# GpSimd's multiplies and scalings wait, by a semaphore, for VectorE's last one ahead of them

## The chip, the cores and the metric

The kernel runs on one core of a Trainium2 chip. The metric is the device time of one execution in microseconds (us). The core's engines are TensorE (PE in the profile, its weight loads PEld), VectorE (DVE), ScalarE (ACT), GpSimd (POOL) and SyncE (SP), which issues the DMAs. Each engine takes its instructions strictly in the order in which they stand, and halts at one whose semaphores have not reached the counts that it waits for.

## What is computed

One transformer block with modulation, for 2048 tokens of width 512, in bfloat16. The reference, cut to what matters:

```python
mod = (silu(c) @ w_mod).reshape(1, 6, 1, 512)            # sa, ca, ga, sb, cb, gb
h = layernorm(x) * (1 + ca) + sa
q, k, v = split(h @ wqkv)                                # 32 heads of 16
pq, pk = q @ w_phi, k @ w_phi                            # per head, 16 x 16
phi_q = concat([softmax(pq), softmax(-pq)])              # over the 16 features
phi_k = concat([softmax(pk), softmax(-pk)])
kv = einsum('sf,sd->fd', phi_k, v);  z = phi_k.sum(0)    # per head, over all tokens
o = (phi_q @ kv) / (phi_q @ z + 1e-6)
x = x + ga * (o @ wo)
h = layernorm(x) * (1 + cb) + sb
x = x + gb * ((sigmoid(h @ w_gate) * (h @ w_up)) @ w_down)   # 512 -> 1376 -> 512
```

## The kernel before

The 2048 tokens are 16 tiles of 128. For each tile t the first half of the program normalises the tokens (`st1`, `rs1`, `nmr1`, `xn1`), transposes them and applies the modulation (`hm1_gj`: unit g of one or two tiles, quarter j of the width), giving `h1T`. TensorE then makes `K`t and `V`t, and `Q`t, 4 matmuls each, into PSUM banks. The feature map of a K tile is: `e`t, two exponentials on ScalarE (for pk and -pk) from the bank into a buffer; `n`t, the sums on VectorE; `r`t, the reciprocals, on VectorE or ScalarE; `phi`t, the product of the two, on VectorE or GpSimd; then `kv`t on TensorE adds phi times V into two accumulating banks. `va`t copies V out of its bank. Of a Q tile it is `qe`t, `qn`t, two products `qphi`t.0 and `qphi`t.1, and `pT`t, a DMA of SP that transposes the result. The names may have a suffix for a part of a tile.

When all of kv is there, `kvz` and `kvn` on VectorE bring it into SBUF, and each tile goes through `num` (TensorE), `rd` and `u` (VectorE), `oT`, `out` (TensorE), `x1` and the second layer norm, `mod` (the second modulation), and then the gated network in six chunks: `g` and `u` on TensorE, `tg` on ScalarE, `hm` on VectorE, `y` on TensorE, `fin`. `wo`j and `wd`j multiply the weights of the two projections by ga and gb beforehand, with both inputs in SBUF.

Every such step is a task of a graph. The order of all tasks is written out by hand as a text, ORDER, one word for each, with @A, @D or @P where the engine is not the first of its alternatives. `emit` goes through it and records each task on its engine; so the text fixes the order on every engine. The framework adds a semaphore wait wherever data, or the reuse of a buffer, needs one. Buffers are slots by class, handed out in the order of the text: all of `e`, `qe`, `phi` and `qphi` share the class r2k, which has 7 slots. A task that takes over a slot waits for its last reader. PSUM has 8 banks, two of them held by kv until its end.

A task has a `port`: the engines on which it counts as an instruction with two inputs in SBUF, or as a scaling of SBUF data. For `phi`, `qphi`, `wo`, `wd`, `xn1`, `xn2`, `mod` and `hm1` these are VectorE and GpSimd (`hm1` and `mod` only where a DMA did the transposing), for all others GpSimd alone. For instance:

```python
G.add(f"phi{t}.{a}", {"POOL": 0.08 + 1.77 * w, "DVE": 0.16 + 0.54 * w}, f_p, r=[("kr", t, a)], w=[("phi", t, a)], bufs=[ee, kr, ph], port=("POOL", "DVE"))
```

The stretch of ORDER around the first place that the prediction speaks of (`phi4.0` on VectorE stands ahead of `qphi1.1` on GpSimd):

```
K7b qe4.0 n4.0 V6 va6 r4.0@A n5.0 V5 va5 tph81 V4 qn4.0 phi4.0@D qphi1.1@P pT2 r5.0@A va4 qphi1.0@P
```

Of the kernel before, what the change touches and what calls it, by code (L numbers as in the profile page):

```python
# [160 lines left out]
def kernel(  # L161
# [4 lines left out]
    nc = tc.nc  # L166
# [91 lines left out]
    def get(b):  # L258
        if b.tile is None:
            pl = psp if b.cls == "bank" else cst  # L260
            b.tile = pl.tile(b.shape, b.dtype, name=b.name, tag=f"{b.cls}{b.slot}", bufs=1)
        return b.tile
# [5 lines left out]
        return Buf(name if name in CAPS else "ks", shape, FP32, name)  # L268

    def emit(order):  # L270
        for t in order:
            for b in t.bufs:
                if b.cls not in ("h2", "hm", "vaug"):
                    get(b)
            t.fn(t.eng)


    def kv_tasks(G, acc, t, ph, va, parts):
# [598 lines left out]
    bound_tasks(G)  # L877
    downstream(G)
    emit(G.arrange(ORDER))

    def gen_tile(tag, shape, dtype, name):
# [177 lines left out]
```

## Time and profile before

| | us |
|---|---|
| median of 3 runs | 203.47 |
| lowest, highest | 203.35, 204.83 |
| profiled execution, first to last instruction (its span) | 202.2 |
| PE busy, of the span | 194.4 (96%) |
| DVE busy | 160.6 (79%) |
| ACT busy | 105.3 (52%) |
| POOL busy | 104.2 (52%) |

The profile is of one execution. For it the span is what is recorded; the timed runs have their whole time, whose median is 1.27 us above the span. The busy shares are means over the whole span, in which the engines have very different parts: the keys' and queries' features come first, the gated network last. The timeline of an engine gives, for groups of like instructions that follow each other, the start, the time from the first one's start to the last one's end, and in brackets the idle time ahead and what ended it. "L784" is line 784 of the kernel before.

### The profile page before, as it was taken

How to read it: one execution, taken by the hardware profiler on the slowest of the kernel's cores; microseconds unless marked ns; L12 is line 12 of the kernel's file. 1: busy time of each engine (PE TensorE's matmuls, PEld its weight loads, DVE VectorE, ACT ScalarE, POOL GpSimd, SP SyncE). 2: the span in 40 equal slices, each digit the busy share in tenths (PEclk: the TensorE clock that was granted, in tenths of full speed). 3: DMA queues.
4: the chain of work that ended last, by engine and by line, in shares of the span. 5: the costliest groups of instructions: out<-in, count | busy, mean ns of one | idle time of the engine just before them, and what ended most of it. 6: DMA issues, size and time to landing. Idle time of an engine off the chain costs nothing.

```text
span 202.2 us, 4128 instructions
## 1 busy us (share of the span) xinstructions
PE 194.4 (96%) x1447; PEld 106.2 (53%) x1471; DVE 160.6 (79%) x376; ACT 105.3 (52%) x250; POOL 104.2 (52%) x146
## 2 busy tenths in 40 slices
PE   7989999999989999999999999999999999999993
PEld 2545656455464787668844444444444444444442
DVE  3999999999999999998897796885969753326622
ACT  2899999999978975576531215212113420334100
POOL 3889978799699998867570066130030431000000
PEclk9999999999999999999999999999999999999999
DMA  5999965669963992418664243542113031000011
GB/s 169 329 262 239 289 232 111 114 71 261 396 254 77 133 109 51 82 39 108 117 79 80 53 79 85 100 104 52 26 26 81 2 78 54 28 5 26 28 54 57
DMA packets 49452, 22.92 MB, mean 113 GB/s; under 512 B 38065, under 2 KB 47634, under 8 KB 49426
## 3 DMA queue, kind: packets, MB, share of 16 engines
q1 hardware_dynamic: 48896, 22.59, 50.1%
q8 instruction: 12, 0.20, 0.4%
q14 instruction: 14, 0.11, 0.2%
q10 hardware_dynamic: 530, 0.02, 0.2%
HBM read 11.58 MB, written 2.10 MB: 68 GB/s over the span
## 4 chain that ended last, share of the span: by engine, by line
PE 70%; ACT 15%; DVE 8%; issue 2%; POOL 2%; DMA 1%; POOLq 0%; DVEq 0%
PE y_ps L485 19%; PE u_ps L447 18%; PE g_ps L447 18%; PE a_ps L356 5%; ACT h1T L751 3%; ACT e L776 3%; ACT qe L776 2%; PE num L326 2%; PE k_ps L817 2%; DVE qks L780 2%; ACT wqk_f L685 2%; PE v_ps L821 2%; DVE ks L780 1%; DMA x_sb<-in_A_x_dram 1%; DVE phi L787 1%
## 5 line engine op out<-in xcount | busy, mean ns | idle before, releaser
L457 ACT ACTIVATE tg<-g_ps 128x512 bf16<-128x512 f32 (+5 forms) x66 | 28.7, 455 | 66.8 <-PE g_ps L447 39.9
L468 DVE SCALAR_TENSOR_TENSOR wmod_sb<-tg,u_ps 128x512 bf16<-128x512 bf16 (+4 forms) x63 | 30.2, 491 | 18.0 <-ACT tg L457 11.5
L485 PE MATMUL y_ps<-wd_sb,wmod_sb 128*128 128x512 bf16 (+4 forms) x180 | 44.2, 366 | 0.2
L447 PEld LDWEIGHTS <-wg_sb 128*128 128x128 bf16 (+1 forms) x252 | 21.9, 99 | 16.1 <-issue 0.2
L447 PEld LDWEIGHTS <-wu_sb 128*128 128x128 bf16 (+1 forms) x252 | 21.7, 99 | 15.9 <-issue 0.3
L784 POOL TENSOR_TENSOR qphi<-qe,qks 128x512 bf16<-128x512 bf16 x24 | 25.1, 1064 | 4.1 <-DMA pT<-qphi 1.4
L485 PEld LDWEIGHTS <-wmod_sb 128*128 128x128 bf16 (+1 forms) x187 | 17.1, 98 | 16.0 <-issue 0.6
L447 PE MATMUL u_ps<-wT_sb,wu_sb 128*128 128x512 bf16 (+2 forms) x124 | 23.8, 322 | 0.1
L447 PE MATMUL g_ps<-wT_sb,wg_sb 128*128 128x512 bf16 (+2 forms) x122 | 23.0, 321 | 0.2
L447 PE MATMUL g_ps<-wqk_sb,wg_sb 128*128 128x128 bf16 (+4 forms) x127 | 19.9, 287 | 0.1
L447 PE MATMUL u_ps<-wqk_sb,wu_sb 128*128 128x128 bf16 (+4 forms) x127 | 19.8, 286 | 0.2
L780 DVE TENSOR_REDUCE ks<-e 128x64 f32<-128x1024 bf16 (+2 forms) x22 | 19.3, 904 | 0.2
L492 DVE TENSOR_TENSOR ot<-y_ps,x 128x512 bf16<-128x512 f32 (+2 forms) x17 | 11.1, 654 | 10.1 <-PE y_ps L485 10.1
L780 DVE TENSOR_REDUCE qks<-qe 128x64 bf16<-128x1024 bf16 x16 | 19.1, 1204 | 0.0
L376 POOL TENSOR_SCALAR ve<-mv 128x2 f32<-128x2 f32 (+1 forms) x8 | 1.8, 226 | 33.4 <-DVE mv L366 33.3
L776 ACT ACTIVATE e<-k_ps 128x512 bf16<-128x512 f32 (+2 forms) x44 | 18.3, 536 | 0.0
L776 ACT ACTIVATE qe<-q_ps 128x512 bf16<-128x512 f32 x32 | 17.1, 612 | 0.8 <-POOL phi L787 0.6
L787 POOL TENSOR_TENSOR phi<-e,kr 128x1024 bf16<-128x1024 bf16 (+2 forms) x10 | 14.9, 1501 | 2.5 <-DVE phi L787 1.2
L817 PE MATMUL k_ps<-wqk_f,h1T 128*128 128x512 bf16 x61 | 16.1, 379 | 0.1
L356 PE MATMUL a_ps<-wo_sb,oT 128*128 128x512 bf16 x60 | 15.9, 379 | 0.2
L871 PE MATMUL q_ps<-wqk_f,h1T 128*128 128x512 bf16 x61 | 15.7, 379 | 0.2
L821 PE MATMUL v_ps<-wv_sb,h1T 128*128 128x512 bf16 x61 | 15.3, 379 | 0.1
(132 smaller groups left out, 307.7 us busy)
## 6 DMA issues: line engine op xcount, KB each, us to landing
out_dram<-ot SPq DMA_DIRECT2D x15, 128.0 KB, 1.8
x_sb<-in_A_x_dram SPq DMA_DIRECT2D x6, 256.0 KB, 5.1
wmod_sb<-in_w_mod_dram SPq DMA_DIRECT2D x1, 1536.0 KB, 7.0
wu_sb<-in_B_w_up_dram SPq DMA_DIRECT2D x1, 1376.0 KB, 10.9
wg_sb<-in_B_w_gate_dram SPq DMA_DIRECT2D x1, 1376.0 KB, 10.3
wd_sb<-in_B_w_down_dram SPq DMA_DIRECT2D x1, 1280.0 KB, 7.9
wmod_sb<-in_w_mod_dram SPq DMA_DIRECT2D x4, 256.0 KB, 6.2
wqk_sb<-in_A_wqkv_dram SPq DMA_DIRECT2D x2, 256.0 KB, 4.8
```

What stands on the lines that cost most here:

```text
L356: pe.matmul(ap_[:], lhsT=oT[:, j, :], rhs=wo_sb[:, j, :], start=(j == 0), stop=(j == KT - 1))
L447: pe.matmul(ps[:fsz, 0:n], lhsT=w[:, j, ft * P:ft * P + fsz], rhs=h[:, j, 0:n], start=(j == 0), stop=(j == KT - 1))
L457: G.add(f"tg{k}.{ft}", {"ACT": 0.13 + n * 0.00083}, lambda e, tg=tg, g_ps=g_ps, fsz=fsz, n=n: act.activation(tg[:fsz, 0:n], g_ps[:fsz, 0:n ...
L468: dve.scalar_tensor_tensor(hm_all[:fsz, hm[k].slot, ft, 0:n], tg[:fsz, 0:n], 1.0, u_ps[:fsz, 0:n], op0=ALU.add, op1=ALU.mult)
L485: mm = pe.matmul(y[:, 0:c1 - c0], lhsT=hm_all[:fsz, hm[k].slot, ft, tl * P:(tl + 1) * P], rhs=wd_sb[:fsz, ft, c0:c1], start=(ft == 0), sto ...
L776: act.activation(ee[:, a:b, s].rearrange("p g f h -> p g (f h)"), kp[:, a * 64:b * 64].rearrange("p (g n) -> p g n", n=64), ACT.Exp, scale ...
L780: dve.tensor_reduce(ks[:, a:b].rearrange("p g s h -> p (g s) h"), ee[:, a:b].rearrange("p g s f h -> p (g s) h f"), axis=AX.X, op=ALU.add)
L784: engine(e).tensor_tensor(ph[:].rearrange("p (g s f h) -> p g s f h", s=2, f=DH, h=4)[:, :, s], ee[:, :, s], ks[:, :, 1 - s].unsqueeze(2). ...
L787: engine(e).tensor_tensor(ph[:, a * P:b * P].rearrange("p (g f h) -> p g f h", f=DH, h=4), ee[:, a:b].rearrange("p g s f h -> p (g s) f h" ...
L817: pe.matmul(kp[:], lhsT=h1T[:, j, t * P:(t + 1) * P], rhs=wqk_f[:, j, D:2 * D], start=(j == 0), stop=(j == KT - 1))
L821: pe.matmul(vp[:], lhsT=h1T[:, j, t * P:(t + 1) * P], rhs=wv_sb[:, j, :], start=(j == 0), stop=(j == KT - 1))
L871: pe.matmul(qp[:], lhsT=h1T[:, j, t * P:(t + 1) * P], rhs=wqk_f[:, j, 0:D], start=(j == 0), stop=(j == KT - 1))
```

## The change

`emit` remembers the last instruction of the last task that went to VectorE with VectorE in its `port`. Ahead of each task of GpSimd with GpSimd in its `port` (but for the small `rs` tasks), it adds a dependency of that task's first instruction on the remembered one. No instruction is added, removed or moved on any engine.

```diff
     def emit(order):
+        last = None
         for t in order:
             for b in t.bufs:
                 if b.cls not in ("h2", "hm", "vaug"):
                     get(b)
+            body = nc.cur_bb.bb.instructions
+            n0 = len(body)
             t.fn(t.eng)
+            if t.eng in t.port and not t.name.startswith("rs"):
+                if t.eng == "DVE":
+                    last = body[-1].name
+                elif last:
+                    tc.add_manual_dep(body[n0], last, mybir.DependencyInfo(mybir.DependencyClass.Sync, mybir.DependencyReason.DATA), reason="port order")
```

VectorE raises its semaphore as it goes on, and GpSimd's tasks wait for a count of it. Where an earlier wait of GpSimd already covers the new dependency, nothing is added. In the built program nine instructions are left whose count is new or higher:

| GpSimd's instruction | its start in the profile before | now waits for VectorE's | which ran |
|---|---|---|---|
| qphi1.1 | 33.43 | phi4 | 36.78 to 37.46 |
| hm1_73 | 43.35 | phi7 | 43.89 to 44.57 |
| wo1 | 49.02 | phi10 | last of three, to 51.34 |
| wo0 | 56.56 | phi12 | to 55.70 |
| mod21 | 87.36 | qphi10.0 | 86.24 to 86.65 |
| xn2_6 | 91.57 | xn2_7 | 91.25 to 91.80 |
| qphi8.1 (second of the pair) | 101.7 | qphi13.0 | 102.53 to 103.05 |
| mod51 | 132.01 | mod50 | 132.97 to 133.32 |
| mod80 (last of four) | 167.2 | mod71 | 166.70 to 167.34 |

GpSimd's row at the first place, before. qphi_800 is the product of tile 1's query, qphi_821 that of tile 4, h1T the modulated input of tiles 10 to 13, phi_833 the feature map of tile 5:

```order
L784 TENSOR_TENSOR qphi_800<-qe_700,qks_755 128x8x64 [waits DVE_49,Activation_49]
L784 TENSOR_TENSOR qphi_800<-qe_700,qks_755 128x8x64
L753 TENSOR_SCALAR h1T_73<-h1T_73,modc_78 128x256 [waits DMAHW2_49,DMAHW1_49]
L753 TENSOR_SCALAR h1T_73<-h1T_73,modc_78 128x256
L784 TENSOR_TENSOR qphi_821<-qe_766,qks_796 128x8x64 [waits DVE_49,PE_49,Activation_49]
L787 TENSOR_TENSOR phi_833<-e_708,kr_804 128x1024 [waits DMAHW4_49,PE_49,Activation_49]
```

And after the change:

```order
L792 TENSOR_TENSOR qphi_800<-qe_700,qks_755 128x8x64 [waits DVE_49,Activation_49]
L792 TENSOR_TENSOR qphi_800<-qe_700,qks_755 128x8x64
L761 TENSOR_SCALAR h1T_73<-h1T_73,modc_78 128x256 [waits DMAHW2_49,DMAHW1_49]
L761 TENSOR_SCALAR h1T_73<-h1T_73,modc_78 128x256
L792 TENSOR_TENSOR qphi_821<-qe_766,qks_796 128x8x64 [waits PE_49,Activation_49]
L795 TENSOR_TENSOR phi_833<-e_708,kr_804 128x1024 [waits DMAHW4_49,PE_49,Activation_49]
```

The wait on VectorE's semaphore at the first row had the count 76 and has the count 80 now, that of phi4; qphi_821, which waited for 80 by itself, is covered by it. Nothing else differs in these rows.

ScalarE's row of e6, the exponentials of tile 6, the same before and after: it takes over the slot of qe_700, and its wait on GpSimd's semaphore (Pool) is for the second qphi_800. ScalarE's e7 takes over the slot of qphi_800 itself, and so waits for the DMA pT1 that reads it. The bank that e6 reads, k_ps_739, is taken over by V9.

```order
L776 ACTIVATE e_837<-k_ps_739 128x8x64 [waits Pool_49]
L776 ACTIVATE e_837<-k_ps_739 128x8x64
```

GpSimd's rows at the second and third place, before. The first h1T here is hm1_73, wo_sb is wo1, and phi_1094 belongs to tile 14:

```order
L753 TENSOR_SCALAR h1T_73<-h1T_73,modc_78 128x256
L787 TENSOR_TENSOR phi_959<-e_857,kr_880 128x1024 [waits PE_49,Activation_49,Pool_49]
L787 TENSOR_TENSOR phi_986<-e_872,kr_936 128x1024 [waits DMAHW3_49,DVE_49,Pool_49]
L787 TENSOR_TENSOR phi_1015<-e_875,kr_938 128x256 [waits DVE_49,Pool_49]
L851 TENSOR_TENSOR wo_sb_68<-wo_sb_68,ga_sb_102 128x512 [waits DMAHW1_49,DMAHW0_49]
L787 TENSOR_TENSOR phi_1094<-e_912,kr_994 128x512 [waits DMAHW5_49,DVE_49]
```

And after the change:

```order
L761 TENSOR_SCALAR h1T_73<-h1T_73,modc_78 128x256 [waits DVE_49]
L795 TENSOR_TENSOR phi_959<-e_857,kr_880 128x1024 [waits PE_49,Activation_49,Pool_49]
L795 TENSOR_TENSOR phi_986<-e_872,kr_936 128x1024 [waits DMAHW3_49,DVE_49,Pool_49]
L795 TENSOR_TENSOR phi_1015<-e_875,kr_938 128x256 [waits DVE_49,Pool_49]
L859 TENSOR_TENSOR wo_sb_68<-wo_sb_68,ga_sb_102 128x512 [waits DMAHW1_49,DMAHW0_49,DVE_49]
L795 TENSOR_TENSOR phi_1094<-e_912,kr_994 128x512 [waits DMAHW5_49,Activation_49]
```

The wait for phi10 has moved from phi_1094 to wo1, which stands one ahead of it, and hm1_73 has a wait where it had none.

## Prediction

> **What bounds the kernel now.** I read the page first, then the busy times by stretch, then the timelines of each engine between 30 and 58 us, where the change has its first effect. The engines' busy times, and two stretches (length, then PE, PEld, DVE, ACT and POOL busy, clock, DMA share, GB/s):
>
> ```profile
> PE 194.4 (96%) x1447; PEld 106.2 (53%) x1471; DVE 160.6 (79%) x376; ACT 105.3 (52%) x250; POOL 104.2 (52%) x146
> ```
>
> ```profile
> 38.00:43.00 5.00, 4.94 (x38) 2.42 (x38) 4.93 (x7) 4.97 (x13) 4.80 (x4) 1.00 0.60 78
> 58.00:200.00 142.00, 139.68 (x942) 75.94 (x955) 106.93 (x253) 52.98 (x114) 56.29 (x73) 1.00 0.35 66
> ```
>
> TensorE is the bound from end to end: from 58 to 200 us it is idle for 2.32 of 142 us, so what is lost ahead of 58 us can't be made up behind it. In the stretch from 38 to 43 us there is no spare engine at all: PE, DVE and ACT are each busy for over 4.9 of 5 us, POOL for 4.8. An engine that halts here passes its halt to the others. That GpSimd is only 52% busy over the span says nothing about this stretch.
>
> **Which added waits hold anything.** Nine instructions of GpSimd get a condition that no earlier wait of theirs covers. GpSimd's timeline (start, time, line, instruction, count, idle time ahead) at the first three:
>
> ```profile
> 33.43 2.08 POOL L784 TENSOR_TENSOR qphi<-qe,qks 128x512 bf16<-128x512 bf16 x2 [0.84 <-DVE qphi L784]
> 35.49 1.10 POOL L753 TENSOR_SCALAR h1T<-h1T,modc 128x256 bf16<-128x256 bf16 x2
> 37.64 1.20 POOL L784 TENSOR_TENSOR qphi<-qe,qks 128x512 bf16<-128x512 bf16 x1 [1.05 <-DVE phi L787]
> 38.80 1.91 POOL L787 TENSOR_TENSOR phi<-e,kr 128x1024 bf16<-128x1024 bf16 x1
> ...
> 43.35 0.56 POOL L753 TENSOR_SCALAR h1T<-h1T,modc 128x256 bf16<-128x256 bf16 x1
> 44.22 4.84 POOL L787 TENSOR_TENSOR phi<-e,kr 128x1024 bf16<-128x1024 bf16 x3 [0.30 <-PE kvacc L282]
> 49.02 1.22 POOL L851 TENSOR_TENSOR wo_sb<-wo_sb,ga_sb 128x512 bf16<-128x512 bf16 x1
> 51.42 3.06 POOL L787 TENSOR_TENSOR phi<-e,kr 128x512 bf16<-128x512 bf16 x3 [1.18 <-DVE phi L787]
> ```
>
> The first row, the fifth and the seventh are the ones that wait (the pair of qphi1, hm1_73, wo1). Of VectorE they now wait for the phi at 36.78, the one at 43.89 and the last of the three from 50.26; with those, the instructions that the working needs:
>
> ```profile
> 36.78 0.68 DVE L787 TENSOR_TENSOR phi<-e,kr 128x1024 bf16<-128x1024 bf16 x1
> ...
> 38.48 2.34 DVE L780 TENSOR_REDUCE ks<-e 128x64 f32<-128x1024 bf16 x2
> ...
> 43.89 0.68 DVE L787 TENSOR_TENSOR phi<-e,kr 128x1024 bf16<-128x1024 bf16 x1
> ...
> 48.87 0.33 DVE L787 TENSOR_TENSOR phi<-e,kr 128x256 bf16<-128x256 bf16 x1
> ...
> 50.26 1.08 DVE L787 TENSOR_TENSOR phi<-e,kr 128x256 bf16<-128x256 bf16 x3
> ...
> 54.05 0.33 DVE L798 RECIPROCAL kr<-ks 128x32 bf16<-128x32 f32 x1
> ```
>
> **First wait: qphi1 on GpSimd waits for phi4 on VectorE.** The pair at 33.43 must now wait until the phi that starts at 36.78 is done. That phi doesn't depend on the pair, so its time stays. It already released a GpSimd instruction, the one at 37.64; the pair will start there instead: 37.64 - 33.43 = 4.21 us later. GpSimd's idle 1.05 us ahead of 37.64 is used up by this, but its 2.08 and 1.10 us of work now come behind the phi. The first qphi at 37.64 lasted 1.20 beside VectorE's qphi instead of its usual half of 2.08, so the pair ends at 37.64 + 1.16 (to the next start, 38.80) + 1.04 = 39.84, where it ended at 35.51.
>
> Who waits for the pair: ScalarE's exponentials e6, which write the buffer that the pair read (its slot is shown with the change, above), and all that stands behind them. ScalarE's and TensorE's timelines:
>
> ```profile
> 36.90 1.09 ACT L776 ACTIVATE e<-k_ps 128x512 bf16<-128x512 f32 x2
> ...
> 39.81 1.12 ACT L776 ACTIVATE e<-k_ps 128x512 bf16<-128x512 f32 x2
> ```
>
> ```profile
> 37.92 0.42 PE L282 MATMUL kvacc<-vaug,phi 128*128 128x68 bf16 x8
> 38.17 1.89 PE L821 MATMUL v_ps<-wv_sb,h1T 128*128 128x512 bf16 x8
> ...
> 43.88 1.02 PE L817 MATMUL k_ps<-wqk_f,h1T 128*128 128x512 bf16 x4
> ...
> 57.38 0.80 PE L326 MATMUL num<-kvb,pT 128*128 128x68 bf16 x20 [0.43 <-DVE kvb L294]
> ```
>
> e6 started at 36.90; it will start at 39.84 and a handover (0.08 from 51.34 to 51.42, the ends of two rows above), so 3.0 us later, and end at 41.0 instead of 37.99. V9, at 38.17, writes the bank that e6 reads out: TensorE, which takes its instructions in order, halts there for 41.05 - 38.17 = 2.9 us. VectorE's sum of e6 started at 38.48, 0.49 after e6 was done; it loses 3.0 - 0.49 = 2.5 us at once, and the rest with the following sums, since ScalarE has no gap in which to catch up. The halt is thus 3.0 us on all three, 2.5 if VectorE alone counted.
>
> The queue of SP is also behind the pair: the transposing DMA of qphi1, and all that SP issues after it.
>
> ```profile
> 35.53 1.23 SPq L874 DMA_TRANSPOSE pT<-qphi  x1
> ```
>
> ```profile
> DMA to landing us min/median/max: 3.2/3.3/3.9
> ```
>
> It goes out at 39.88 instead of 35.53 and lands 3.2 later, at 43.1. The exponentials e7 reuse its source buffer: they start at 39.81, with the shift 42.81, so they wait 0.3 more. **3.3 us** by now.
>
> **Second wait: hm1_73 waits for phi7 on VectorE.** GpSimd went from its phi straight to hm1_73 at 43.35; the phi of VectorE ends at 44.57. GpSimd is then 3.0 behind, VectorE 3.3, so hm1_73 starts at 44.57 + 3.3 + 0.15 (a handover like that to 37.64) = 48.0 and not at 46.4. Of the 1.6 us, the idle 0.30 ahead of 44.22 takes some, and GpSimd is about 4.4 behind. TensorE's K at 43.88 reads hm1_73 with its last quarter (at 44.53): ready at 48.6, so TensorE stands 4.1 back there, which it partly makes up later, as it isn't what the num at 57.38 waits for. VectorE's phi at 48.87 waits for the second of GpSimd's three phis from 44.22, which by its share of the elements (4.84 x 2 / 2.25 = 4.3) ends at 48.5: slack 0.4. It is thus pushed by 4.4 - 0.4 = 4.0, against 3.3: 0.7 more, of which I take 0.2 off, since the first of the three overlaps VectorE's phi from 43.89 now and won't then: **0.5 us**.
>
> **Third wait: wo1 waits for phi10 on VectorE.** wo1 filled GpSimd's idle time ahead of 51.42, where the next phi was released by the very phi that wo1 now waits for (50.26 + 1.08 = 51.34). Now wo1's 1.2 us come between. Two of GpSimd's three phis from 51.42 are done after 3.06 x 2/3 = 2.04, at 53.46; VectorE's reciprocal at 54.05 waits for them with a slack of 0.59: 1.2 - 0.6 = **0.6 us** more. From there VectorE sets the num at 57.38 (the wait named in its row), and PE halts until it comes.
>
> **The later waits.** At 56.56 the wo0 is ready late anyway, and the mod at 87.36 finds its VectorE instruction done. The others hold GpSimd for 0.1 to 1.4 us:
>
> ```profile
> 100.69 2.08 POOL L784 TENSOR_TENSOR qphi<-qe,qks 128x512 bf16<-128x512 bf16 x2 [0.58 <-POOL wT_sb L424]
> ...
> 132.01 1.73 POOL L424 TENSOR_SCALAR wqk_sb<-wqk_sb,modc 128x256 bf16<-128x256 bf16 x3 [1.42 <-issue]
> ```
>
> ```profile
> 102.53 0.52 DVE L784 TENSOR_TENSOR qphi<-qe,qks 128x512 bf16<-128x512 bf16 x1
> ```
>
> ```profile
> 132.97 0.35 DVE L422 TENSOR_SCALAR wqk_sb<-wqk_sb,modc 128x256 bf16<-128x256 bf16 x1
> ```
>
> ```profile
> 109.49 0.44 PE L326 MATMUL num<-kvb,pT 128*128 128x68 bf16 x8
> 135.50 1.03 PE L447 MATMUL g_ps<-wqk_sb,wg_sb 128*128 128x512 bf16 x4
> ```
>
> The second qphi8 at 101.7 waits until 103.05: 1.4 later, out at 104.2, landed by 108.1 at the slowest, and its reader comes at 109.49. The three mods from 132.01 wait until 133.32: done at 135.1, their reader comes at 135.50. I take both at nothing; if the covers were gone they would cost 0.3 each.
>
> **What the waits save.** VectorE sometimes finds GpSimd on the port. Its qphi and its mod, over the whole program (min/median/max ns):
>
> ```profile
> L784 DVE TENSOR_TENSOR qphi<-qe,qks x8: 415/416/518, 32.5 to 114.0; 128x512 bf16<-128x512 bf16 x8
> ```
>
> ```profile
> L422 DVE TENSOR_SCALAR wqk_sb<-wqk_sb,modc x1: 347/347/347, 133.0 to 133.0; 128x256 bf16<-128x256 bf16 x1
> L422 DVE TENSOR_SCALAR wT_sb<-wT_sb,modc x1: 637/637/637, 166.7 to 166.7; 128x256 bf16<-128x256 bf16 x1
> ```
>
> One qphi in eight is longer, by 0.10 us; one mod by 0.29. With as much for the forms not shown, 0.5 us at most, nearly all behind 58 us where PE is full without it: I take 0. The Trainium skill's page "SBUF — State Buffer", section "Who interferes with whom", states that a VectorE instruction with two SBUF inputs or in a 2-port mode and a reading GpSimd instruction exclude each other for the whole instruction, whoever starts first. The rows agree in kind, and by the rule alone this change should win; by these rows the sum would be 4.4 - 0.5 = 3.9.
>
> **Sum.** 3.0 + 0.3 + 0.5 + 0.6 = 4.4 us on the profiled span of 202.2: 206.6. The median of the runs shown is 203.47, 1.27 above that span, for what lies around it: 206.6 + 1.3 = **207.9 us**.
>
> **Rivals.**
> - *The first wait alone costs* (chance 0.21). For it: the second and third terms rest on slacks of 0.5 us read from a stage that will have shifted. Against: the rows show no other spare time. 2.5 to 3.3 us: 206.0 to 206.8.
> - *The delayed GpSimd clashes more* (0.14). With GpSimd late, its phis start as VectorE's phis at 48.87 and 54.3 become ready, both from one release. A blocked VectorE waits for a phi like those of 51.42's row (3.06 / 3 = 1.02 each); two of them, with GpSimd's tail taken off, add 1 to 1.7: up to 209.6.
> - *TensorE's clock drops in the halt* (0.05). The first matmuls of the program against K's in the middle:
>
> ```profile
> 1.25 2.74 PE L600 MATMUL warm<-wd_sb 128*128 128x512 bf16 x6 [1.25 <-DVE wd_sb L593]
> ...
> 4.12 2.74 PE L600 MATMUL warm<-wd_sb 128*128 128x512 bf16 x6
> ```
>
>   Six take 2.74, some 0.43 each with the last one's tail; four K take 1.02, some 0.21 each. A clock that falls back at 41 us, for the 5.6 us from 1.25 to 6.86 that it is slow at the start, costs 2.8 us of TensorE, of which its halt ahead of the num hides 0.43 + 0.5 + 0.6 = 1.5: 209.2. For: the halt is 2.9 us. Against: no later row shows a halt of over 1 us, so nothing shows that it would. The skill's page "TensorE: Matmul & The Clock Gate", section "Why this matters for your kernels", says that a pause of over about 3 us halves the clock; no run here shows where that point lies.
> - *Relief of VectorE wins* (0.04, other side: faster). VectorE paces the stage, and the waits keep GpSimd off the port as it is about to need it. It decides if e6 doesn't need the pair's buffer, so that the delayed pair is covered; then the 0.5 us above is gained at most, partly: 203.0. Against: e6 started right when ScalarE was free, but its wait on GpSimd's count stands in the order.
> - *The delay is absorbed* (0.05): only if TensorE could run other work in the halt; it takes its work in order. 203.5 to 205.4.
>
> **Numbers.** The forecast itself has 0.51, with 207.0 to 208.7 as its own range. The range from 205.8 to 209.6 takes in the first two rivals and most of the clock's, and leaves out under 0.15. About 1%, 2 us, is what a measurement of this kernel can tell from no change. Slower by over that: 0.51 + 0.21 + 0.14 + 0.05 = 0.91; within it 0.06; faster 0.03, as relief would give only 0.5.
>
> **What would show it.** In the profile of the changed kernel: qphi at about 37.6 after some 5 us of idle GpSimd, put down to VectorE's phi; ScalarE idle for 2.9 us ahead of an e; TensorE with a hole of that length at 38.2, nothing of the kind later; the num from 57.38 at about 61.8, and all behind it shifted alike. If ScalarE's e still starts at 36.9, the first term is wrong and with it the forecast; if the hole is there but the num comes before 60.7, the second and third are.

## The result, and the profile after

The changed kernel takes 209.75 us (median of 6 runs, 208.93 to 210.29), the kernel before 203.41 (6 runs, 203.18 to 204.83): 1.030 times as long, with a 95% interval of 1.027 to 1.032. It is slower, as forecast; 209.75 lies 1.85 above the forecast, 1.05 above that forecast's own range and 0.15 above the whole range.

The profiled execution of after took 209.82 us, with a span of 207.9 against 202.2. Its engines:

```profile
PE 194.3 (93%) x1447; PEld 106.0 (51%) x1471; DVE 162.0 (78%) x376; ACT 105.6 (51%) x250; POOL 103.4 (50%) x146
```

The work is the same (TensorE 194.3 and 194.4 us); what has come in is idle time. Where, the timelines show (start, time, engine, line, instruction, count, idle time ahead and what ended it; each line number is 8 higher than before). GpSimd, after:

```profile
37.92 2.24 POOL L792 TENSOR_TENSOR qphi<-qe,qks 128x512 bf16<-128x512 bf16 x2 [5.02 <-DVE phi L795]
...
48.09 0.56 POOL L761 TENSOR_SCALAR h1T<-h1T,modc 128x256 bf16<-128x256 bf16 x1 [1.33 <-DVE phi L795]
48.61 4.70 POOL L795 TENSOR_TENSOR phi<-e,kr 128x1024 bf16<-128x1024 bf16 x3
55.06 1.16 POOL L859 TENSOR_TENSOR wo_sb<-wo_sb,ga_sb 128x512 bf16<-128x512 bf16 x1 [1.74 <-DVE phi L795]
56.18 4.24 POOL L795 TENSOR_TENSOR phi<-e,kr 128x512 bf16<-128x512 bf16 x4
61.38 3.40 POOL L859 TENSOR_TENSOR wo_sb<-wo_sb,ga_sb 128x512 bf16<-128x512 bf16 x3 [0.96 <-DVE phi L795]
```

The waits of qphi1, hm1_73, wo1 and wo0 (rows one, two, four and six) are all there, each put down to a phi of VectorE. ScalarE behind the first of them, after:

```profile
40.19 1.09 ACT L784 ACTIVATE e<-k_ps 128x512 bf16<-128x512 f32 x2 [2.87 <-POOL qphi L792]
...
43.26 1.08 ACT L784 ACTIVATE e<-k_ps 128x512 bf16<-128x512 f32 x2
```

TensorE, after, and one row of TensorE before at the same work:

```profile
35.48 0.28 PE L752 MATMUL tp_h<-ident,xn 128*128 128x128 bf16 x2
...
41.33 1.89 PE L829 MATMUL v_ps<-wv_sb,h1T 128*128 128x512 bf16 x8 [2.68 <-ACT e L784]
...
48.70 0.39 PE L825 MATMUL k_ps<-wqk_f,h1T 128*128 128x512 bf16 x1 [0.60 <-POOL h1T L761]
...
61.36 1.19 PE L290 MATMUL kvacc<-vaug,phi 128*128 128x68 bf16 x32 [1.50 <-DVE phi L795]
62.99 0.92 PE L334 MATMUL num<-kvb,pT 128*128 128x68 bf16 x24 [0.44 <-DVE kvb L302]
```

```profile
35.18 0.28 PE L744 MATMUL tp_h<-ident,xn 128*128 128x128 bf16 x2
```

At 35.2, ahead of every added wait, this execution is 0.30 later already; that is its start, and is taken off in what follows ("net of the start": each profile's times less what its tp_h is later than 35.18). V9 is 2.86 later (41.33 - 38.17 - 0.30), num 5.31 (62.99 - 57.38 - 0.30), and the end 5.4 (207.9 - 202.2 - 0.30). From num on nothing more is lost: from 64 to 205 us TensorE is idle for 1.7 of 141 us.

VectorE, after, where the second part of the loss arises:

```profile
41.31 1.22 DVE L788 TENSOR_REDUCE ks<-e 128x64 f32<-128x1024 bf16 x1 [2.43 <-ACT e L784]
...
47.31 0.68 DVE L795 TENSOR_TENSOR phi<-e,kr 128x1024 bf16<-128x1024 bf16 x1
...
52.55 0.29 DVE L795 TENSOR_TENSOR phi<-e,kr 128x256 bf16<-128x256 bf16 x1 [0.18 <-POOL phi L795]
...
53.89 1.08 DVE L795 TENSOR_TENSOR phi<-e,kr 128x256 bf16<-128x256 bf16 x3
...
58.26 0.35 DVE L806 RECIPROCAL kr<-ks 128x32 bf16<-128x32 f32 x1 [0.46 <-POOL phi L795]
58.53 2.77 DVE L795 TENSOR_TENSOR phi<-e,kr 128x512 bf16<-128x512 bf16 x3
```

The phi at 52.55 is 3.38 later than at 48.87, the reciprocal at 58.26 3.91 later than at 54.05. The last row is VectorE's last three phis (phi13.0, phi15.0, phi12.0). Their times in the view of that tile, min/median/max in ns, in before and in after:

```profile
L787 DVE TENSOR_TENSOR phi<-e,kr x3: 412/452/679, 54.3 to 55.0; 128x512 bf16<-128x512 bf16 x2, 128x1024 bf16<-128x1024 bf16 x1
```

```profile
L795 DVE TENSOR_TENSOR phi<-e,kr x3: 679/980/1262, 58.5 to 60.6; 128x512 bf16<-128x512 bf16 x2, 128x1024 bf16<-128x1024 bf16 x1
```

The larger third one is as before (679). The two smaller ones went from 0.45 and 0.41 to 0.98 and 1.26 us: 1.4 us, and this is just what num is later than the reciprocal (5.31 - 3.91). GpSimd's four phis of the same shape run from 56.18 to 60.42 without a gap beside them. Before, the fourth came at 55.14 after 0.66 us of idle time, when these two of VectorE were done.

So the balance of the profile: 0.3 start, 2.9 the first wait, 1.0 what comes on top by the reciprocal, 1.4 the two long phis.

### The profile page after: what moved, and what is told of

The parts are those of the page before. It is cut to its first block, busy times and chain, and to the rows that moved or that the text cites. A ratio compares the mean times of both kernels' runs of the same rounds, so it can differ in the third digit from the quotient of the medians.

```text
span 207.9 us, 4129 instructions
## 1 busy us (share of the span) xinstructions
PE 194.3 (93%) x1447; PEld 106.0 (51%) x1471; DVE 162.0 (78%) x376; ACT 105.6 (51%) x250; POOL 103.4 (50%) x146
## 4 chain that ended last, share of the span: by engine, by line
PE 66%; ACT 15%; DVE 5%; DMA 5%; issue 4%; POOL 2%; SPq 2%; POOLq 0%; ACTq 0%; DVEq 0%
PE y_ps L493 18%; PE u_ps L455 17%; PE g_ps L455 17%; PE a_ps L364 5%; ACT e L784 4%; ACT h1T L759 3%; DMA wmod_sb<-in_w_mod_dram 3%; ACT qe L784 2%; PE num L334 2%; ACT vaug L844 2%; DVE qks L788 2%; DMA pT<-qphi 1%; POOL phi L795 1%; PE g_ps L457 1%; PE q_ps L879 1%
```

## Experiments

Each run is the kernel before or after with the edit that is named. To select a wait, `emit` remembers the VectorE task's name as well, and adds the dependency only if that name fits:

```diff
-                    last = body[-1].name
-                elif last:
+                    last, of = body[-1].name, t.name
+                elif last and of == "phi4.0":
```

**The first wait alone** (qphi1 for phi4; the edit above).

> Of the added waits only the first is kept: qphi1 on GpSimd waits for phi4 on VectorE. Theory (the terms of the sum, and on top of them a clash of GpSimd's and VectorE's phis near 58 us that needs GpSimd to come later against VectorE than before): 3.0 + 0.3 us over the kernel before, 206.4 to 206.9, with VectorE's phi13.0 and phi15.0 as short as before (0.45 and 0.41). Rival (the first halt alone brings about the clash as well): over 208, with these two near 1 and 1.3 us.

Measured: 208.02 us (206.31 to 208.34), 1.019 times before [1.013, 1.025]. The runs are of two kinds: one of 206.31 with a mean granted clock of 1.0, and three of 207.83 to 208.34 with 0.99. The first, a single run, is what the theory said. The profile of one of the others shows no clash at the last phis (1.39 us as before), but this at TensorE's hole (timeline, and the windows' columns: length, PE, PEld, DVE, ACT and POOL busy, granted clock, DMA share, GB/s):

```profile
59.13 1.39 DVE L795 TENSOR_TENSOR phi<-e,kr 128x512 bf16<-128x512 bf16 x3
```

```profile
41.79 3.29 PE L829 MATMUL v_ps<-wv_sb,h1T 128*128 128x512 bf16 x8 [2.68 <-ACT e L784]
```

```profile
41.70:43.00 1.30, 1.21 (x3) 0.40 (x3) 1.22 (x1) 1.30 (x4) 1.30 (x3) 0.50 0.97 179
43.00:45.00 2.00, 2.00 (x7) 0.77 (x6) 1.68 (x2) 1.51 (x4) 2.00 (x2) 0.59 0.81 89
45.00:48.00 3.00, 2.95 (x22) 1.47 (x22) 2.44 (x3) 2.94 (x11) 1.69 (x2) 1.00 0.35 77
```

After the hole the eight matmuls of V9 and V7 take 3.29 us and not 1.89: the granted clock is 0.50 until about 44.65, and TensorE loses 1.4 us. Not all of it arrives: num comes at 62.21, and with the start of this execution taken off (its tp_h came at 35.98, 0.80 late) that is 4.03 later than before, where the same wait without a fall of the clock made it 3.1 (the run with the hole filled, below). Of these 0.9 us, 0.4 are VectorE's three phis ahead of the reciprocals, which take 1.50 beside wo1 and not 1.08.

**All waits but the first** (`of != "phi4.0"`).

> All added waits but the first. Theory: GpSimd is some 1 us late behind hm1_73 and another 1.2 behind wo1, VectorE takes 0.4 and 0.6 of it, and then the clash of the phis adds up to 1.4: 204.4 without the clash, 205.8 with all of it. Rival (the later waits cost only because everything is late by the first): 203.4.

Measured: 206.58 us (205.36 to 207.31), 1.013 [1.007, 1.018]. The three phis of VectorE take 2.77 us again, with no delay of GpSimd from the first wait. In the profiled execution, of 207.31, num came at 59.35, which is 2.21 later net of the start (0.24 early): 0.81 up to the reciprocal and 1.40 of the two phis, where 2.4 was worked out. At num the clock fell as well, 0.50 from 59.1 to 62.6, and the span is 3.4 longer, net. The fastest run, 205.36, has a mean clock of 1.0 and is near the 205.8 of the working; two more whose clock held (0.999 and 1.0) took 206.25 and 206.92. Why these are longer isn't shown; the runs of before at the same time, with clocks of 0.997 and more, spread as far (203.19 to 204.89).

```profile
54.89 2.77 DVE L795 TENSOR_TENSOR phi<-e,kr 128x512 bf16<-128x512 bf16 x3
```

**All waits but the third** (`of != "phi10.0"`).

> All added waits but the third, wo1's for phi10. Theory: first and second cost 3.3 + 0.4, and without wo1's 1.2 us ahead of GpSimd's last phis these stand to VectorE's as before, so no clash: 207.0 to 207.4, phi13.0 and phi15.0 on VectorE 0.45 and 0.41. Rival (the clash comes from the first halt or from the second wait): 208.5 or more, with them near 1 and 1.3 us.

Measured: 208.19 us (207.49 to 209.1), 1.023 [1.017, 1.029]. No clash at the last phis, as the theory said. The one run whose clock held (1.0) took 207.49, 0.1 above what was expected; the three others, with 0.992, took 208.17 to 209.1. In the profile the clock falls behind a hole of the same 2.68 us, and the eight matmuls of V9 and V7 take 3.52 us.

```profile
58.72 1.39 DVE L795 TENSOR_TENSOR phi<-e,kr 128x512 bf16<-128x512 bf16 x3
```

```profile
40.78 3.52 PE L829 MATMUL v_ps<-wv_sb,h1T 128*128 128x512 bf16 x8 [2.68 <-ACT e L784]
```

**The later waits alone** (`of not in ("phi4.0", "phi7.0", "phi10.0")`).

> Without the first three waits: the six from wo0's on alone. Theory: they cost nothing, 203.4 within 0.4, and VectorE's longer qphi (0.52) and mod (0.64) are 0.42 and 0.35. Rival (relief of VectorE is worth something): 203.0 or less; rival (their covers are too thin): 203.9 or more.

Measured: 203.56 us (10 runs), 1.0002 [0.998, 1.003]. The later waits cost nothing, and what they save is nothing too, although VectorE's qphi is now never long (its slowest of 8 is 424 ns, 518 before):

```profile
L792 DVE TENSOR_TENSOR qphi<-qe,qks x8: 359/416/424, 32.2 to 113.7; 128x512 bf16<-128x512 bf16 x8
```

Its long mod was expected at 0.35 us and stays at 0.62 (637 ns before, 611 in after): of GpSimd's four mods only the last waits for it, and the third, which ends at 166.89, still runs when it starts at 166.34.

**After, with GpSimd's last phi put behind.** In ORDER `phi15.4`, GpSimd's last, goes behind VectorE's `phi12.0`, for which it then waits:

```diff
- ... phi15.4 r15.0 va14 phi13.0@D phi15.0@D Q5 phi12.0@D ...
+ ... r15.0 va14 phi13.0@D phi15.0@D Q5 phi12.0@D phi15.4 ...
```

> The change, and GpSimd's last phi of tile 15 (the second of the two that start at 58.49 and after in the profile after) is put behind VectorE's phi12 in the order, so that by the new rule it waits for it. Theory, the clash: in the profile after, VectorE's phi13.0 and phi15.0 took 0.98 and 1.26 us beside GpSimd's phis and not 0.45 and 0.41; without GpSimd's last phi beside them phi15.0 is back near 0.41 (phi13.0 stays long beside the one ahead), num comes 0.3 to 0.85 earlier than at 62.99 and the whole is 208.6 to 209.2. Rival, VectorE is long for another reason, or num waits for GpSimd's phi instead: phi15.0 stays over 1 us, or num stays at 63.0: 209.5 or more.

Measured: 208.77 us (208.58 to 208.94), 1.023 [1.017, 1.029], where after had 1.030. VectorE's three phis:

```profile
L795 DVE TENSOR_TENSOR phi<-e,kr x3: 414/679/982, 58.8 to 60.1; 128x512 bf16<-128x512 bf16 x2, 128x1024 bf16<-128x1024 bf16 x1
```

phi15.0 is back at 0.41 and phi13.0 is still 0.98. So it is GpSimd's phi beside it that made it long. That num came earlier for it this profile doesn't show: 62.45 is 0.54 before the 62.99 of after, but this execution started 0.54 earlier too (tp_h at 34.94 against 35.48). Its clock fell at 41.8, and with that VectorE's last three phis begin 0.85 later than in after, net of the starts (58.84 and 58.53), which is just what phi15.0 no longer loses (1.26 - 0.41). The runs show the gain: all four have a mean clock of 0.992, and their 208.77 is 1.26 below the 210.03 of the three runs of after with 0.991 to 0.992.

**The third wait alone** (`of == "phi10.0"`), **and the same with GpSimd's last phi put behind** (that edit, and `of in ("phi10.0", "phi12.0")`).

> Only the wait of wo1 for phi10. Theory, the clash is this wait's child: wo1 goes ahead of phi14, GpSimd's phis reach past VectorE's last three, and phi13.0 and phi15.0 take 0.98 and 1.26 us; num is later by 0.6 (the slack, as in the prediction) and 1.4 (the clash): 205.4, and up to 206.7 where the granted clock falls ahead of num as in the run with all waits but the first. Rival, the clash needs the second wait or the late stage too: VectorE's three phis take 1.4 us as in the kernel before, and the whole is 204.0.

> Only the wait of wo1 for phi10, and GpSimd's last phi of tile 15 behind VectorE's phi12 in the order, for which it waits. Theory: phi15.0 at 0.41 us again, phi13.0 still 0.98, so num is later by 0.6 + 0.5 = 1.1: 204.5, up to 205.5 where the clock falls. Rival, GpSimd's later phi sets num in its place: as late as with the wait of wo1 alone.

Measured: 207.59 us (207.04 to 209.06), 1.019 [1.017, 1.022], and 204.68 us (204.42 to 204.97), 1.006 [1.004, 1.008]. VectorE's three phis with the third wait alone:

```profile
L795 DVE TENSOR_TENSOR phi<-e,kr x3: 981/1264/1641, 55.2 to 57.3; 128x512 bf16<-128x512 bf16 x2, 128x1024 bf16<-128x1024 bf16 x1
```

The wait of wo1 makes the clash by itself: 0.98 and 1.26 as in after. It is even worse here, since the third phi is long too, 1.64 and not 0.68: without a wait of its own, wo0 starts while it runs. GpSimd's row:

```profile
57.05 4.03 POOL L859 TENSOR_TENSOR wo_sb<-wo_sb,ga_sb 128x512 bf16<-128x512 bf16 x3
```

In after wo0 waits for that phi. So one of the added waits does what such a wait can do, and saves 0.96 us, in a place that another one made late. That, and the clock, which is 0.50 for 6.8 us (58.3 to 65.1) from within a hole of 3.02 us ahead of the sums of kv on, put this run above what was expected of it (TensorE, and two of the windows):

```profile
58.98 2.00 PE L290 MATMUL kvacc<-vaug,phi 128*128 128x68 bf16 x32 [3.02 <-DVE phi L795]
```

```profile
58.98:60.50 1.52, 1.51 (x27) 1.52 (x28) 1.24 (x3) 1.08 (x2) 1.52 (x2) 0.50 0.72 284
...
62.50:64.50 2.00, 1.78 (x11) 0.93 (x10) 2.00 (x5) 0.00 (x0) 1.74 (x2) 0.50 0.00 0
```

With the last phi put behind, and wo0 waiting for phi12 as in after, no clash but phi13.0 is left and the clock holds in every run: 204.68, where 204.5 was worked out. num is 1.13 later net of the start (58.31, with a tp_h at 34.98), as the sum of 0.6 and 0.5 said.

```profile
54.70 1.92 DVE L795 TENSOR_TENSOR phi<-e,kr 128x512 bf16<-128x512 bf16 x3
```

**The second wait alone** (`of == "phi7.0"`).

> Only the wait of hm1_73 for phi7. Theory: 1.1 us of GpSimd that its idle time and VectorE's slack take up, 203.4 to 203.8. Rival, it carries the 0.5 us that the prediction gave it, and it brings the clash: 204 to 205.4.

Measured: 203.83 us (10 runs), 1.0018 [0.9999, 1.0037]: 0.4 us by the ratio, 0.75 at most by its interval. In the profile num is 0.68 later net of the start (57.65, with a tp_h at 34.77). Of this 0.24 is there when the row below begins (50.09 against 50.26), and the rest is another small clash: the phis that took 1.08 us from 50.26 before take 1.51, as wo1 starts beside them. In after wo1 waits for them and they are 1.08 again.

```profile
50.09 1.51 DVE L795 TENSOR_TENSOR phi<-e,kr 128x256 bf16<-128x256 bf16 x3
```

**Eight slots in place of seven** in the class of e, qe, phi and qphi, in before and in after (`"r2k": 8`), so that e6 takes over another slot than that of the delayed pair.

> The kernel before with 8 slots in place of 7 in the class that e, qe, phi and qphi share: the control to the next run. Both theories: the buffers do not bound the kernel before, 203.4 within 0.4.

> The change with 8 slots in place of 7 in that class, so that e6 no longer takes over the slot that the delayed pair of qphi1 reads. Theory, the first term passes by that one slot: ScalarE's e6 starts near 36.9 again, TensorE has no hole at 38.2, and what is left is that of the run with all waits but the first: 205.4 to 206.6. Rival, the pair's delay of GpSimd (3 us late for its phis) passes on by the phis that the keys' sums need, whatever the slot: a hole appears a few us later and the time is 208 or more.

Measured: 206.13 us (205.59 to 206.35), 1.011 [1.004, 1.017], and 209.88 us (208.86 to 210.49), 1.027 [1.020, 1.034]. Neither is what was expected. The control is no control: with eight slots the slots fall to other tasks, and in before the pair of qphi1 itself waits for a transposing DMA and starts 2.05 us later. GpSimd and TensorE of before with eight slots:

```profile
35.48 2.53 POOL L784 TENSOR_TENSOR qphi<-qe,qks 128x512 bf16<-128x512 bf16 x2 [3.39 <-DMA pT<-qphi]
```

```profile
42.20 0.43 PE L282 MATMUL kvacc<-vaug,phi 128*128 128x68 bf16 x8 [1.66 <-POOL phi L787]
```

In after with eight slots e6 does start at 36.6 and V9 has no hole; the hole comes 4 us further on, where kv needs GpSimd's phi:

```profile
36.63 1.08 ACT L784 ACTIVATE e<-k_ps 128x512 bf16<-128x512 f32 x2
...
39.42 1.08 ACT L784 ACTIVATE e<-k_ps 128x512 bf16<-128x512 f32 x2 [1.21 <-POOL qphi L792]
```

```profile
43.41 0.63 PE L290 MATMUL kvacc<-vaug,phi 128*128 128x68 bf16 x8 [2.07 <-POOL phi L795]
```

So the rival holds for the hole: the slot is the first way by which the delay passes, not the only one. V9 is no longer late, and yet TensorE waits for one of GpSimd's own phis; ScalarE's next e, at 39.42, waits for a qphi, so the way by the slot is not gone either. The time of this run isn't the price of that alone: the clock is 0.50 for 6.8 us from within this hole on, and VectorE's phi of 45.13 takes 2.10 us beside GpSimd's. The two runs differ by 3.75 us, against 6.3 with seven slots, but in the first of them the pair is 2 us late by itself.

**The first wait alone, with TensorE's hole filled.** A task ahead of `V9` in ORDER; its sums go to columns that nobody reads:

```diff
+    def f_fill(e):
+        for _ in range(24):
+            pe.matmul(kvacc[0][:, 4 * HC:512], lhsT=ident[:], rhs=wqk_f[:, 0, 0:512 - 4 * HC], start=False, stop=False, skip_group_check=True)
+    G.add("fill", {"PE": 2.4}, f_fill, bufs=[kvacc[0]])
```

> The first wait alone, and 24 matmuls of 240 columns, whose sums go to columns that nobody reads, put on TensorE ahead of V9, where its hole is (240 of the 512 columns of a K matmul, whose step is some 0.21 us: 0.1 us each, 2.4 us in all, an estimate). Theory, the granted clock falls because TensorE stands still: it stays at 1.0 in every run, and the runs lie at 206.3 within 0.4 like the one run of the first wait alone whose clock stayed. Rival, the clock falls for another reason: the runs lie at 206.3 and at 207.8 to 208.3 again, with mean clocks of 0.99 in these.

Measured: 209.24 us (208.89 to 210.88), 1.024 [1.018, 1.031]. The profile shows what the fill was for, and why the time is not what was expected:

```profile
38.23 2.62 PE L851 MATMUL kvacc<-wqk_f,ident 128*128 128x240 bf16 x24
41.08 1.89 PE L829 MATMUL v_ps<-wv_sb,h1T 128*128 128x512 bf16 x8 [0.22 <-ACT e L784]
...
60.57 0.93 PE L334 MATMUL num<-kvb,pT 128*128 128x68 bf16 x24 [0.43 <-DVE kvb L302]
...
82.15 1.04 PE L364 MATMUL a_ps<-wo_sb,oT 128*128 128x512 bf16 x4 [1.16 <-DMA oT<-o]
```

V9 and V7 take 1.89 us at the full clock, and num comes 3.1 later net of the start (60.57 against 57.38, with a tp_h at 35.26), as the theory said. Behind num, however, TensorE waits for transposes that landed late: the one of oT issued at 77.9 took 4.2 us to land, where 2.5 is usual before (the median of the four from 70 to 84 us).

By 82.15 TensorE is 5.5 us late. The other runs lie at 208.9 to 209.5 with mean clocks of 0.996 to 1.0, so they lost much the same without a clock that falls; the 0.994 of the profiled one comes from behind the last matmul (0.58 from 206.0 to 209.2). Why these transfers were late wasn't found. For the clock, one filled hole and one clock that held is what this run gives; its time says nothing about it.

## Why the prediction was right, and where it was short

The direction was right and so was the first term, step by step; the time lies 0.15 us above the top of the whole range. The step that failed is the third wait's, which ends at a reciprocal and leaves out the clash behind it.

**The first wait (3.0 us): right, step by step.** The pair started when phi4 was done, after 5.02 us of idle time; ScalarE stood 2.87 us ahead of an e, TensorE had a hole of 2.68 us where 2.9 was worked out, VectorE's sum waited 2.43 (2.5 in the working). V9 came 2.86 later, net of the start. The one run with this wait alone whose clock held was 2.8 above before (206.31 against 203.51), and with the hole filled num was 3.1 later. That the delay passes by the pair's buffer was right for this order but too narrow: with eight slots TensorE waits for GpSimd's own phi.

**The DMA and the second wait (0.3 + 0.5): too much.** The places came as said: hm1_73 waited 1.33 us, and K's last quarter waited for it, at 48.4 net of the start (48.6 forecast). But VectorE's phi7, on which all of this hangs, was 3.1 late and not 3.3 (47.31 against 43.89, net): ScalarE's e7 started 0.15 later still and not 0.3 (43.26 against 39.81, 3.15 net, on 3.0). So GpSimd was 4.1 behind at its phi of 48.61, and not 4.4, and the phi at 52.55 is 3.38 later where the sum has 3.8. The second wait alone made the phis at that place 0.24 later.

**The third wait (0.6): right at its place, and short by its consequence.** The reciprocal was 0.53 later on top. But the prediction stopped at that reciprocal and let VectorE run on from there as before. It had the mechanism as a rival, "the delayed GpSimd clashes more", with 1 to 1.7 us; it came, with 1.4. Its cause was put too generally: it isn't that GpSimd is late (with the first wait alone, or with all but the third, these phis take 1.39 us as before; with the third alone the clash is there), but wo1, which goes ahead of GpSimd's phis and leaves no gap before the last of them. The rows of before would have shown it: wo1 behind the phi of 51.34 ends at 52.6, GpSimd's four phis of 1.05 behind it at 56.8, and VectorE's three start 0.6 later than at 54.31, at 54.9. In both pairs GpSimd's phi had begun first:

```profile
58.19 1.04 POOL L795 TENSOR_TENSOR phi<-e,kr 128x512 bf16<-128x512 bf16 x1
59.19 1.23 POOL L795 TENSOR_TENSOR phi<-e,kr 128x512 bf16<-128x512 bf16 x1
```

```profile
58.53 0.98 DVE L795 TENSOR_TENSOR phi<-e,kr 128x512 bf16<-128x512 bf16 x1
...
59.44 1.86 DVE L795 TENSOR_TENSOR phi<-e,kr 128x512 bf16<-128x512 bf16 x2
```

phi13.0 started at 58.53 and phi15.0 at 59.44, beside the first and the second of these two. The Trainium skill, page "SBUF — State Buffer", section "Who interferes with whom", says that a VectorE instruction with two SBUF inputs contends with a GpSimd instruction that reads SBUF, and that what they share is held as an exclusive lock. The rows agree: phi15.0 ended at 60.70, 0.28 after GpSimd's phi beside it, and with GpSimd's last phi put behind, 1.26 became 0.41.

**The saving (0): right for the program, not in kind.** The later waits gave 1.0002. In the stage up to num two waits did shorten VectorE's phis, by 0.96 us (wo0's, 1.64 to 0.68) and 0.4 (wo1's, 1.51 to 1.08), both times only after another wait had made GpSimd late: in the kernel before these phis are as short.

**The clock: given 0.05, and it fell in half of the runs of after.** They have mean clocks of 0.998 to 0.999 in three runs (208.93, 209.41, 209.82) and 0.991 to 0.992 in the other three (209.68, 210.03, 210.29): 0.6 us apart by their medians. The working said 5.6 us at half the clock, 2.8 us of TensorE, 1.5 of it hidden ahead of num. Where a profile shows a fall behind this hole, it lasts 3.4 us (last section, with what decides whether it comes), so it costs TensorE 1.7 at most (1.40 and 1.63 in the two rows of V9 and V7), and 0.9 of that was seen at num, VectorE having been held up too. No profile of after has a fall, so how much of it that kernel hides isn't shown.

**What lies around the span (1.3): 0.6 too small.** The prediction took the median less the span of one execution. In after it is 1.9 (209.82 - 207.9). The span of before that was profiled had a late start: in the run with the later waits alone, whose span was 201.6, the tp_h of 35.18 came at 34.81. Among the profiles with seven slots the start differs by 1.2 us (34.77 to 35.98), so single runs that lie less than that apart show little.

Together: 207.9 - 0.5 (chain) + 1.4 (clash) + 0.6 (around the span) + 0.3 (start) = 209.7, for a profiled execution of 209.82. The term that was mis-sized is the third wait: 0.6 where 0.5 + 1.4 was measured, the 1.4 being the clash, and with it the likeliest case: the forecast's mechanism and this rival are not two ways to go, both happened. That the total is not further off is in part luck, since the 0.5 too much in the chain hid a third of the clash.

## What to carry to other kernels

A semaphore between two engines that share something costs what the waiting engine's slack doesn't cover, and the waiting engine is late for all that follows. Before adding one, follow its lateness to the next place where the two engines meet: the wait that keeps them apart here can put them on top of each other there. Where an engine that is late is waited for in two ways, taking away the first wait can move the hole and not remove it, as with eight slots here.

## What was not expected of the hardware

The same hole of TensorE, 2.68 us, stands in four profiles. In after the granted clock stays at 1.00 behind it; with the third wait left out, and with GpSimd's last phi put behind, it falls to 0.50. Windows of the three, in this order:

```profile
41.30:43.00 1.70, 1.68 (x8) 0.78 (x8) 1.38 (x2) 1.70 (x4) 1.70 (x2) 1.00 0.88 164
```

```profile
42.00:44.00 2.00, 2.00 (x6) 0.71 (x5) 1.68 (x2) 1.56 (x4) 2.00 (x2) 0.50 0.81 87
```

```profile
42.00:44.00 2.00, 2.00 (x7) 0.62 (x6) 1.75 (x3) 1.93 (x5) 2.00 (x2) 0.50 0.79 83
```

With the first wait alone (shown above) it is 0.50 too. It began 0.55 us before the hole's end in that run (at 41.24) and 1.0 after it in the third of these (at 41.78, the hole's end being at 40.74). So the hole's length alone doesn't decide: the same kernel has the fall in some executions and not in others, with times of 207.83 to 208.34 against 206.31, of which the start makes part (it was 0.80 late in the 208.34).

What decides can be read from the thirteen traces kept. Each records when the granted clock changes, and within a trace all these times lie whole multiples of 3.413 us apart: with the first wait alone the clock is full from 7.11 us for ten such steps, 0.50 for one, and full again for 48. With TensorE's idle time counted by these steps, every step up to the last matmul with 1.74 us of it or more is followed by one at 0.50: 1.74 (all but first), 1.85 (after with eight slots), 2.13 (first alone), 2.31 (third alone), 2.39 (last phi put behind), 2.68 (all but third). No step with 1.66 (before with eight slots) or less is. In after a step ends at 39.91, in the midst of the hole, and leaves 1.26 us of idle time in one step and 1.41 in the next: the clock held. So what halves the clock here is a step of which TensorE idles over about half, and where the steps lie against the program differs from execution to execution. With eight slots and with the third wait alone the clock stayed at 0.50 for a second step, the first having 0.85 and 0.72 us of idle time; where it recovered at once, that had 0.55 at most. A mean clock of 0.992 or 0.984 is thus one step at 0.50 or two.

The Trainium skill, page "TensorE: Matmul & The Clock Gate", section "Part 1: The HAM clock gate (the "warmup" mystery)", says that activity is measured over windows of about 3.4 us that run free of the kernel, which these steps bear out. That it takes one whole idle window doesn't fit as written: half of one was enough.
